# Output matmuls of a fused attention and maxout kernel issued as four column-tiled matmuls of 32 tokens

## The chip, the cores and the metric

The kernel runs on one core of one Trainium2 chip. The metric is the device time of one launch in microseconds (us), lower is better. The kernel before took 325.02 us, the median of two runs (324.05 and 326.00).

## The reference

Two stages over 4 batches of 12544 tokens with 128 channels, 32 inducing points and a maxout layer of width 1024 behind them:

```python
def mab(q, kv):
    s = scale * (q @ kv.transpose(0, 2, 1))
    s = s - s.max(-1, keepdims=True)
    a = np.exp(s)
    a /= a.sum(-1, keepdims=True) + 1e-09
    return a @ kv
h = mab(I, x)             # 32 inducing points attend to a batch's tokens
x2 = mab(x, h)            # each token attends to the 32 results
h1 = x2 @ w1
h2 = x2 @ w2
g = np.maximum(h1, h2)
out = g @ w_out           # (50176, 128), float32
```

## The kernel before

The tokens of a batch are cut into 98 chunks of 128. The kernel never forms x2. For each token it makes 32 unnormalised attention weights e (an exponential of scores), and since max(h1, h2) = h1 + max(h2 - h1, 0), the output is e times a small matrix (e @ (h w1 w_out), the "linear term") plus relu(e @ (h (w2 - w1))) @ w_out, all divided by the sum of the weights (the "denominator").

Work on TensorE (PE), in the names of the code:

- `stage` (L610): scores of up to 16 chunks at a time. Four chunks lie side by side in 32 partitions each, so these matmuls use 32 of the 128 columns of the array each, at `tile_position=(0, 32 * q)`: column-tiled. ScalarE (ACT) makes the exponential into a tile `e2`.
- `phase` (L1069): four matmuls (or a few more where they are narrow) that contract over 32 weights each, at `tile_position=(32 * q, 0)`: row-tiled, all four row strips at once. Each fills a bank with 512 columns of h2 - h1, which ACT (L1085) or VectorE (DVE, L1088) rectifies into a `relu` tile in f16. One of the four may be a linear term instead.
- `final_one` (L876): one output matmul, 128 tokens by 128 channels, contracting over 128 of the 1024 units. Its weights (stationary operand) are a 128x128 slice of a `relu` tile, its moving operand is a 128x128 slice of `w_out`. A chunk takes 8 of these, 3136 in all for 392 chunks. Up to four chunks share one bank of 512 columns. When a group is done, DVE scales it by the reciprocal denominators (`evict_group`, L907) and SyncE stores it by DMA.
- `linear_last` (L853): for a few groups ("full") the linear term comes after the output matmuls, one full-array matmul for each chunk.
- `dens` (L671): denominators, one matmul with 4 moving columns for each chunk column of a block. The later blocks get them from a DMA transpose and GpSimd instead.
- `keep_busy` (L833): idle matmuls on zeros, 256 columns each, that add nothing to the bank of a waiting group.
- `pool_scores` (L329) and `pool_accum` (L385, L404): the first attention of the next batch, also column-tiled. L385 is four matmuls side by side, each with 32 columns of weights and 128 moving columns.
- `pool_rest` (L351), `small_rep` (L430), `small_h` (L443), `small_hwd` (L505), `small_m1` (L518): a few matmuls over the full array for each batch.

The program's order on each engine is written out by a planner in the kernel itself: a `Clock` object holds an estimate of when PE, ACT, DVE and each of the 8 banks come free, with constants for an output matmul (0.0558 us) and for a change between full, row-tiled and column-tiled work, and a table of hand-made exceptions (`DEV`). The planner runs while the kernel is built. In the steady state a row-tiled phase and a run of some 13 to 16 output matmuls alternate. The first 25 us (the `HEAD` list) handle the first attention of batch 0 and contain no output matmul.

Of the kernel before, what the change touches and what calls it, by code (L numbers as in the profile page):

```python
# [102 lines left out]
def kernel(  # L103
# [9 lines left out]
    nc = tc.nc  # L113
# [28 lines left out]
    def bank(shape, dtype=F32, only=None):  # L142
        i = min(range(8), key=lambda j: ck.bank[j]) if only is None else only
        uid[0] += 1
        return i, psum.tile(shape, dtype, name=f"ps{uid[0]}", tag=f"bank{i}", bufs=1)
# [47 lines left out]
    repd = consts.tile([128, 128], F32, name="repd")  # L193
    diag = consts.tile([128, M], F32, name="diag")
    pace = consts.tile([128, 1], F32, name="pace")

    with tc.manual_schedule(engines={ET.PE, ET.DVE, ET.Activation, ET.Pool, ET.SP}):

# [457 lines left out]
        def dens(blk):  # L656

            blks = [blk]
            if 0 < blk.index < len(blocks) - 1:
                nxt = blocks[blk.index + 1]  # L660
                if nxt.staged is not None and nxt.staged <= ck.pe and nxt.rp is None and not nxt.turned:
                    blks.append(nxt)
            bi, ps = bank([128, 512])
            ck.wait(ck.bank[bi], "den bank")
            uid[0] += 1
            rp = rpp.tile([128, 8, 4], F32, name=f"rp_{uid[0]}", tag="rp")
            n = 0
            for blk in blks:
                wd = blk.width
                for t in range(wd):  # L670
                    nc.tensor.matmul(  # L671
                        out=ps[:, 4 * (n + t) : 4 * (n + t) + 4],
                        lhsT=blk.e2[:, 128 * t : 128 * (t + 1)],
                        rhs=ones_q,
                        start=True,
                        stop=True,
                    )
                blk.rp = rp[:, n : n + wd, :]
                n += wd
            end = ck.run(0.029 * n)  # L680
            nc.vector.reciprocal(out=rp[:, 0:n, :].rearrange("p t q -> p (t q)"), in_=ps[:, 0 : 4 * n])
            ck.bank[bi] = ck.on_dve(end, 0.18 + 0.001 * 4 * n)
# [138 lines left out]
        def keep_busy(until):  # L821

            g = groups[state["g"]] if state["g"] < len(groups) else None
            if held and held[0].full:
                g = held[0]
            elif g is None or g.ps is None or (g.full and state["mm"] == 0):
                return
            turn = ck.SWITCH["full"] if ck.mode != "full" else 0.0
            n = int((until - ck.pe - turn - 0.1) / 0.11)
            if n < (3 if turn else 1):  # L830
                return
            for _ in range(n):
                nc.tensor.matmul(  # L833
                    out=g.ps[:, 0:256],
                    lhsT=warm[:, 0:128],
                    rhs=warm[:, 0:256],
                    start=False,
                    stop=False,
                    skip_group_check=True,
                )  # L840
            ck.run(0.11 * n)

# [2 lines left out]
        def linear_last(end):  # L845

            while held:
                g = held[0]
                if g.full:
                    if st[g.blk.b].get("m1r", INF) > ck.pe:  # L850
                        return
                    for s, (q, t) in enumerate(g.chunks):
                        nc.tensor.matmul(  # L853
                            out=g.ps[:, 128 * s : 128 * (s + 1)],
                            lhsT=g.blk.e2[:, 128 * t : 128 * (t + 1)],
                            rhs=m1bd[:, q, :],
                            start=False,
                            stop=True,
                            skip_group_check=True,
                        )  # L860
                    end = ck.run(0.056 * len(g.chunks))
                evict_group(held.pop(0), end)

        def final_one():
            g = groups[state["g"]]
            n = len(g.chunks)
            if g.blk.rp is None and not g.blk.turned:
                dens(g.blk)
            if g.ps is None:
                g.bank, g.ps = bank([128, 512])  # L870
                ck.wait(ck.bank[g.bank], "group bank")
                ck.bank[g.bank] = INF
            jb, c = divmod(state["mm"], n)
            q, t = g.chunks[c]
            w4 = g.blk.quarters[q].w
            nc.tensor.matmul(  # L876
                out=g.ps[:, 128 * c : 128 * (c + 1)],
                lhsT=g.blk.relu[q][:, 128 * (jb * w4 + t) : 128 * (jb * w4 + t + 1)],
                rhs=woutp[:, jb, :],
                start=(g.full and state["mm"] == 0),  # L880
                stop=(jb == NJB - 1 and not g.full),
                skip_group_check=True,
            )
            end = ck.run(ck.PAIR)
            state["mm"] += 1
            state["done"] += 1
            if state["mm"] == n * NJB:
                held.append(g)
                linear_last(end)
                state["g"] += 1  # L890
                state["mm"] = 0
# [119 lines left out]
        def phase(jobs):  # L1011
# [6 lines left out]
            for (kind, q, a, u), bi in zip(jobs, free):  # L1018
                _, ps = bank([128, 512], only=bi)
                ready = max(ck.bank[bi], a.blk.staged if kind == "L" else a.staged)  # L1020
                if kind == "L":
                    ready = max(ready, st[a.blk.b]["m1r"])
                got.append((kind, q, a, u, bi, ps, ready))
            keep_busy(max(g[6] for g in got) - ck.SWITCH["row"])
            if ck.mode != "row":
                ck.pe += ck.SWITCH["row"]
# [221 lines left out]
        while state["g"] < len(groups) or held:  # L1248
# [3 lines left out]
            if held and ck.mode == "full":  # L1252
                linear_last(0.0)
# [19 lines left out]
            if tp < INF and lag() <= 128 + LIMIT and now:  # L1273
                if how != 3 and column_work(len(jobs) + 1, how == 4):
                    continue
                phase(jobs)
            elif tf < INF:
                keep_busy(tf)
                ck.wait(tf, "relu")
                final_one()  # L1280
            elif tp < INF:
                phase(jobs)
            elif pending:
                f, a = pending.pop(0)
                f(*a)
            else:
                raise AssertionError(("stuck", state, ptr, chunks_done, jobs, pending[:3]))
# [32 lines left out]
```

## Time and profile before

| what | value |
|---|---|
| times of the two runs | 324.05 us and 326.00 us, median 325.02 us |
| span of the profiled execution, first to last instruction | 322.5 us |
| median of the runs less that span (what lies around it) | 2.5 us |
| granted TensorE clock over the span | 1.000 |
| instructions with a record | 12605, of them 5375 matmuls and 5375 weight loads on PE |

The page gives the span of the profiled execution and not a separate time for it, so the 2.5 us set it beside the median of the runs. "PE" in the profile is the matmuls, "PEld" the weight loads that overlap them. A matmul is pipelined: its record of some 219 ns reaches from the start of its data to the modelled end, so records of neighbours overlap, and the spacing of matmuls is read from the difference of their starts. In a row of the timeline, a length less the length of one record is the time from the first start to the last start. Sources are lines of the kernel before.

### The profile page before, as it was taken

What the parts mean: (1) busy time and instruction counts of PE and PEld (TensorE: products, weight loads), DVE (VectorE), ACT (ScalarE), POOL (GpSimd) and SP (SyncE); (2) the same over time, 40 slices, a digit from 0 to 9 for tenths busy, and PEclk for the clock granted to TensorE, in tenths of its full rate; (3) what the DMA queues carried; (4) which work ended last, traced back from release to release, by engine and by line L of the source; (5) the groups of instructions that cost most, each with busy time, mean ns of one, the idle gap of its engine ahead of it and who ended that gap; (6) DMA issues with size and microseconds to landing.
All of it is one profiled execution on the core that took longest, in us unless ns stands there. A gap on an engine that the chain in (4) does not pass through costs nothing.

```text
span 322.5 us, 12605 instructions
## 1 busy us (share of the span) xinstructions
PE 315.6 (98%) x5375; PEld 239.8 (74%) x5375; DVE 281.4 (87%) x508; ACT 281.8 (87%) x561; POOL 37.8 (12%) x90
## 2 busy tenths in 40 slices
PE   7899999999999999999999999999999999999996
PEld 3776777777777777777777777777777777777786
DVE  3369999988989998999989989988998999899974
ACT  3779999998978999999898999998869999999960
POOL 7470000000040000000040000000006400302000
PEclk9999999999999999999999999999999999999999
DMA  8999999954279999794279999893424322324233
GB/s 205 207 268 213 218 249 203 210 136 133 100 150 245 221 254 216 181 194 139 99 151 242 218 258 207 160 211 120 118 96 103 135 80 100 109 100 128 87 118 116
DMA packets 77320, 53.99 MB, mean 167 GB/s; under 512 B 56112, under 2 KB 64976, under 8 KB 77264
## 3 DMA queue, kind: packets, MB, share of 16 engines
q1 hardware_dynamic: 71232, 39.42, 50.0%
q0 software_dynamic: 5888, 13.70, 21.7%
q8 instruction: 42, 0.69, 0.9%
q14 instruction: 14, 0.11, 0.1%
q10 hardware_dynamic: 144, 0.07, 0.1%
HBM read 27.28 MB, written 25.69 MB: 164 GB/s over the span
## 4 chain that ended last, share of the span: by engine, by line
PE 93%; DMA 5%; ACT 1%; issue 1%; POOL 0%; DVE 0%; POOLq 0%
PE ps L876 62%; PE ps L1069 22%; DMA xn<-in_x_dram 5%; PE ps L610 2%; PE ps L385 2%; PE ps L329 1%; PE ps L671 1%; PE ps L833 1%; ACT e L629 0%; PE ps L505 0%; ACT hwd L482 0%; PE ps L235 0%; PE ps L303 0%; PE ps L430 0%; PE ps L258 0%
## 5 line engine op out<-in xcount | busy, mean ns | idle before, releaser
L1085 ACT ACTIVATE relu<-ps 128x512 f16<-128x512 f32 x462 | 244.1, 604 | 23.0 <-PE ps L1069 15.0
L1088 DVE TENSOR_SCALAR relu<-ps 128x512 f16<-128x512 f32 x322 | 206.1, 682 | 16.2 <-PE ps L1069 14.8
L876 PE MATMUL ps<-woutp,relu 128*128 128x128 f16 x3136 | 216.9, 220 | 0.0
L876 PEld LDWEIGHTS <-relu 128*128 128x128 f16 x3136 | 176.6, 98 | 39.4 <-issue 28.9
L1069 PE MATMUL ps<-e,hwd 32*128 32x512 f16 (+2 forms) x888 | 88.2, 358 | 0.1
L907 DVE TENSOR_TENSOR o<-ps,rp 128x512 f32<-128x512 f32 (+3 forms) x80 | 51.2, 640 | 1.8 <-PE ps L876 1.3
L1069 PEld LDWEIGHTS <-hwd 32*128 32x128 f16 x888 | 24.5, 91 | 20.9 <-issue 0.8
L1069 PE MATMUL ps<-m,e 32*128 32x128 f16 x381 | 38.7, 217 | 0.0
L1069 PEld LDWEIGHTS <-e 32*128 32x128 f16 x381 | 21.2, 92 | 2.9 <-issue 0.4
L907 DVE TENSOR_TENSOR o<-ps,rpt 128x512 f32<-128x512 f32 (+3 forms) x28 | 17.3, 618 | 4.1 <-PE ps L853 2.2
L166 POOL DMA_DIRECT2D xn<-in_x_dram x33 | 17.8, 553 | 6.7 <-DMA xn<-in_x_dram 4.6
L164 POOL COPY pace<-hacc 128x1 f32<-128x1 f32 x2 | 0.4, 188 | 133.1 <-DVE hacc L418 133.1
L246 DVE COPY xT<-ps 128x768 f16<-128x768 f16 (+6 forms) x11 | 4.8, 458 | 8.9 <-PE ps L235 8.9
L340 ACT ACTIVATE eu<-ps 128x512 f16<-128x512 f32 x18 | 10.9, 614 | 0.1
L629 ACT ACTIVATE e<-ps 128x512 f16<-128x512 f32 (+2 forms) x21 | 10.4, 568 | 0.2 <-PE ps L610 0.2
L235 PE MATMUL ps<-identity,xn 128*128 128x128 f16 x98 | 8.1, 219 | 2.3 <-DMA xn<-in_x_dram 1.8
L535 POOL COPY m1bd<-m 32x128 f16<-32x128 f16 x4 | 1.1, 287 | 76.7 <-DVE m L530 76.6
L249 ACT COPY xT<-ps 128x768 f16<-128x768 f16 (+5 forms) x10 | 6.5, 671 | 3.0 <-PE ps L235 2.9
L698 POOL TENSOR_TENSOR w1T<-den 128x256 f32<-128x256 f16 (+1 forms) x7 | 4.4, 633 | 38.6 <-DMA den<-e 38.6
L700 POOL TENSOR_TENSOR w1T<-w1T 128x64 f32<-128x64 f32 (+4 forms) x28 | 8.4, 302 | 2.2
L235 PEld LDWEIGHTS <-xn 128*128 128x128 f16 x98 | 5.6, 97 | 4.0 <-DMA xn<-in_x_dram 2.2
L610 PE MATMUL ps<-xT,hT 128*32 128x512 f16 (+3 forms) x114 | 8.2, 361 | 0.0
(93 smaller groups left out, 117.0 us busy)
## 6 DMA issues: line engine op xcount, KB each, us to landing
out_dram<-o SPq DMA_DIRECT2D x68, 256.0 KB, 2.8
xn<-in_x_dram POOLq DMA_DIRECT2D x24, 448.0 KB, 10.1
out_dram<-o SPq DMA_DIRECT2D x54, 128.0 KB, 1.8
wf<-in_moe_w_dram POOLq DMA_DIRECT2D x4, 256.0 KB, 5.9
xn<-in_x_dram POOLq DMA_DIRECT2D x3, 224.0 KB, 8.8
xT<-xn SPq DMA_TRANSPOSE x42, 3.8
xf<-in_x_dram SPq DMA_DIRECT2D x1, 512.0 KB, 3.7
xf<-in_x_dram SPq DMA_DIRECT2D x1, 384.0 KB, 4.2
```

Source lines behind the costliest of these rows:

```text
L166: nc.gpsimd.dma_start(out=xn_at[b, i][lo:hi, 0:n, :], in_=xr[b, lo:hi, k0 : k0 + n, :])
L235: nc.tensor.transpose(ps[:, j, :], xn_at[0, i][:, g + j, :], identity16)
L249: nc.scalar.copy(out=dst, in_=ps[:, 0:m, :])
L340: nc.scalar.activation(out=eu, in_=ps, func=AF.Exp, scale=scale, accum_out=st[b]["es"][:, u : u + 1])
L610: nc.tensor.matmul(out=ps[32 * q : 32 * (q + 1), 128 * t : 128 * (t + n)], lhsT=hq, rhs=xT[:, c : c + n, :], start=True, stop=True, tile_p ...
L629: nc.scalar.activation(out=blk.e2[:, lo:hi], in_=ps[:, lo:hi], func=AF.Exp, scale=st[0]["rs"] if blk.b == 0 else scale,)
L700: nc.gpsimd.tensor_add(acc[:, :, 0:n], acc[:, :, 0:n], acc[:, :, n : 2 * n])
L876: nc.tensor.matmul(out=g.ps[:, 128 * c : 128 * (c + 1)], lhsT=g.blk.relu[q][:, 128 * (jb * w4 + t) : 128 * (jb * w4 + t + 1)], rhs=woutp[: ...
L907: nc.vector.tensor_mul(osb[:, 0:n, :], g.ps[:, 0 : n * C].rearrange("p (s c) -> p s c", s=n), rp)
L1069: nc.tensor.matmul(**seq[i])
L1085: nc.scalar.activation(out=dst, in_=src, func=AF.Relu)
L1088: nc.vector.tensor_scalar(out=dst, in0=src, scalar1=0.0, scalar2=None, op0=ALU.max)
```

## The change

A helper `by_columns` takes the place of `nc.tensor.matmul` at four places: the output matmul (L876), the late linear term (L853), the denominator (L671) and the idle matmul (L833). It issues four matmuls in place of one. Each takes 32 of the 128 weight columns (32 tokens), the whole moving operand, and writes 32 partitions of the same columns of the same bank. All matmuls of the four places carry `tile_position=(0, 32 * p)`. The planner's constants, the `DEV` table and everything on the other engines are left as they were.

```diff
+    def by_columns(out, lhsT, rhs, start, stop):
+
+        for p in range(4):
+            r = slice(32 * p, 32 * (p + 1))
+            nc.tensor.matmul(
+                out=out[r, :],
+                lhsT=lhsT[:, r],
+                rhs=rhs,
+                start=start,
+                stop=stop,
+                tile_position=(0, 32 * p),
+                skip_group_check=True,
+            )
...
-                    nc.tensor.matmul(
+                    by_columns(
                         out=ps[:, 4 * (n + t) : 4 * (n + t) + 4],
                         lhsT=blk.e2[:, 128 * t : 128 * (t + 1)],
                         rhs=ones_q,
...
-                nc.tensor.matmul(
+                by_columns(
                     out=g.ps[:, 0:256],
                     lhsT=warm[:, 0:128],
                     rhs=warm[:, 0:256],
                     start=False,
                     stop=False,
-                    skip_group_check=True,
                 )
...
-                        nc.tensor.matmul(
+                        by_columns(
                             out=g.ps[:, 128 * s : 128 * (s + 1)],
                             lhsT=g.blk.e2[:, 128 * t : 128 * (t + 1)],
                             rhs=m1bd[:, q, :],
                             start=False,
                             stop=True,
-                            skip_group_check=True,
                         )
...
-            nc.tensor.matmul(
+            by_columns(
                 out=g.ps[:, 128 * c : 128 * (c + 1)],
                 lhsT=g.blk.relu[q][:, 128 * (jb * w4 + t) : 128 * (jb * w4 + t + 1)],
                 rhs=woutp[:, jb, :],
                 start=(g.full and state["mm"] == 0),
                 stop=(jb == NJB - 1 and not g.full),
-                skip_group_check=True,
             )
```

## The prediction

> **What bounds the kernel now.** I read the page's busy line and chain of waits first, then the timeline of PE around 75 to 79 us, where all three kinds of tiling stand side by side, then the list by source for single lines. From the page:
>
> ```profile
> span 322.5 us, 12605 instructions
> PE 315.6 (98%) x5375; PEld 239.8 (74%) x5375; DVE 281.4 (87%) x508; ACT 281.8 (87%) x561; POOL 37.8 (12%) x90
> ...
> q8 instruction: 42, 0.69, 0.9%
> ...
> PE 93%; DMA 5%; ACT 1%; issue 1%; POOL 0%; DVE 0%; POOLq 0%
> ...
> L876 PE MATMUL ps<-woutp,relu 128*128 128x128 f16 x3136 | 216.9, 220 | 0.0
> ```
>
> PE is busy for 98% of the span and carries 93% of the chain that ends last, so what a PE step costs is paid in full, and what other engines do costs nothing while DVE and ACT have 13% to spare. The 3136 output matmuls waited for no data (the last 0.0). The timeline of PE (start, length, line, form, count):
>
> ```profile
> 74.71 0.40 PE L1069 MATMUL ps<-e,hwd 32*128 32x512 f16 x4
> 75.03 0.78 PEld L876 LDWEIGHTS <-relu 128*128 128x128 f16 x14 [0.23 <-issue]
> 75.03 0.95 PE L876 MATMUL ps<-woutp,relu 128*128 128x128 f16 x14
> 75.92 0.09 PEld L1069 LDWEIGHTS <-hwd 32*128 32x128 f16 x2
> ...
> 76.25 0.95 PE L876 MATMUL ps<-woutp,relu 128*128 128x128 f16 x14
> 77.14 0.10 PEld L1069 LDWEIGHTS <-hwd 32*128 32x128 f16 x4
> 77.14 0.40 PE L1069 MATMUL ps<-e,hwd 32*128 32x512 f16 x4
> 77.47 0.90 PEld L385 LDWEIGHTS <-eT 128*32 128x32 f16 x64 [0.23 <-issue]
> 77.47 1.08 PE L385 MATMUL ps<-xn,eT 128*32 128x128 f16 x64
> ...
> 78.47 0.28 PEld L876 LDWEIGHTS <-relu 128*128 128x128 f16 x5
> ```
>
> And by source:
>
> ```profile
> L385 PEld LDWEIGHTS <-eT x288: 92/97/97, 77.5 to 236.8; 128*32 128x32 f16 x144
> L385 PE MATMUL ps<-xn,eT x288: 219/219/230, 77.5 to 236.8; 128*32 128x128 f16 x144
> L385 PEldq EVENT_SEMAPHORE  x3: 51/51/51, 77.1 to 216.0; - x3
> ```
>
> The reader is to see two things. The kernel alternates: a row-tiled phase (L1069), a change of tiling, some 14 output matmuls, a change back, in about 1.2 us. And L385 is already the new form: four matmuls of 32 weight columns and 128 moving columns, side by side, f16, accumulating into one bank.
>
> **The change part by part.**
>
> *Output matmuls, 3136 to 12544.* Before: 14 of L876 start over 0.95 - 0.22 = 0.73 us, 13 gaps of 56 ns. After, by L385: 64 start over 1.08 - 0.22 = 0.86 us, which is 13.7 ns each if spread evenly, 55 ns for four; if the four of a quad start together, 15 gaps of 57 ns. So four cost what one costs, 56 ns, within about -1.5 and +1.0 ns. Times 3136 that is between -5 and +3 us; I take 0, since the same 128 columns stream. The quads differ from L385 in one respect: all four read the same moving operand at once, where each tile of L385 reads its own. No row shows that; I take it at nothing, as the addresses of L385's weights lie side by side in the same way and do no harm.
>
> The weight loads of L385 take 97 ns, those of L876 by the group list 98, and both start ahead of their matmuls; with four loads to a quad, 64 of them start over 0.90 - 0.10 = 0.80 us, in step with the matmuls.
>
> [...]
>
> *Changes of tiling.* From a phase's start to the first output matmul 75.03 - 74.71 = 0.32 us; to the first L385 77.47 - 77.14 = 0.33. From the last output matmul's start (75.03 + 0.73 = 75.76) to the next phase 0.16; from the last L385 (77.47 + 0.86 = 78.33) to the next load of L876 0.14, with a quad's own skew in front. So no change of tiling becomes cheaper or dearer by more than the 0.01 us of the rows. In the order of PE's instructions I count 476 changes before and 478 after: some 30 between column-tiled work and output matmuls go away, since these are now one mode, and some 30 come new around the full-array steps (L351, L430, L443, L505, L518). At 0.32 - 0.22 = 0.10 us each (four times 56 ns is the stream of 512 columns) the two more cost 0.2 us. The fourth matmul of a quad starts a little after the first, so each of the 221 runs ends later by 0 to 0.01 us: 0 to 2.2, I take 1.1 us.
>
> *Denominators, 76 to 304.* The list by line and timelines of three spots:
>
> ```profile
> L671 PE MATMUL ps<-ones_q,e 128*128 128x4 f16 x76 | 3.5, 165 | 0.1
> ```
> ```profile
> 24.92 0.24 PE L671 MATMUL ps<-ones_q,e 128*128 128x4 f16 x4
> ```
> ```profile
> 88.31 0.22 PE L404 MATMUL ps<-xn,et 128*32 128x128 f16 x2
> 88.31 0.17 PE L404 MATMUL ps<-ones,warm 128*32 128x1 f16 x2
> 88.36 0.17 PE L404 MATMUL ps<-ones,et 128*32 128x1 f16 x2
> ```
>
> One denominator now costs (0.24 - 0.164) / 3 = 25 ns. A quad costs between the same 25 (all four side by side) and 56 (a full quad): 0 to 2.4 us over 76. The nearest row is L404, short column-tiled matmuls 50 ns apart: 76 x 25 = 1.9 us, which I take.
>
> *Late linear terms (11) and idle matmuls (13).* These keep their 128 and 256 moving columns, by the quad argument 0. The idle ones fill a wait that exists anyway.
>
> *What supplies the instructions.* PE had 2 x 5375 loads and matmuls. 3136 + 76 + 11 + 13 = 3236 pairs become 12944, so PE now gets 2 x 15083 = 30166, one each 10.7 ns over the span against 30 ns before; in a run of quads, 8 in 56 ns, one each 7 ns. The work that could hide a slow supply is a queue of instructions ahead of the array. The row that bears on it is the semaphore instruction of L385: it waits in PE's queue directly ahead of the first load, at 77.1 us for 0.05. The burst's 128 instructions were therefore handed over between 77.15 and the start of its last load, 77.47 + 0.80 = 78.27: at most 1.1 us / 128 = 9 ns each, and the array never starved. A steady run looks the same: the phase ahead of it gives 0.32 us of lead, then come 13 to 16 quads, as many as L385's 16. At the 9 ns bound a run gains a delay of 72 - 56 = 16 ns for each quad beyond about 16. I take 0.
>
> *Everything else.* No instruction of DVE, ACT, GpSimd or SyncE moves and no DMA is added but fetches of instructions (0.69 MB to about 1.9 MB, 0.9% to 2.6% of the queues' time). A wait on a relu tile or a bank is now met by the first of four, and the scaling of a group waits for the last; both stand within 10 ns of before.
>
> *Sum.* 0 + 0.2 + 1.1 + 1.9 = 3.2 us on a span of 322.5, so 325.7; with the 2.5 us between span and median, **328.2 us**. The bounds of these terms alone are -5 + 0 + 0 + 0 and +3 + 2.2 + 2.2 + 2.4, so 320 to 335; quads at the ends of that are less likely than in the middle, so the own range of this case is 323 to 332.
>
> **The rivals.**
>
> *Supply at the bound.* If an instruction costs 9 ns, runs over 16 quads lose 16 ns a quad. The chain's long runs show the amount:
>
> ```profile
> 306.19 1.78 PE ps L876 x30
> 309.19 2.34 PE ps L876 x40
> 313.96 2.45 PE ps L876 x42
> ```
>
> These three alone lose (14 + 24 + 26) x 16 ns = 1 us; with the rest, and runs at the edge, I put 4 us: 332 us. For it: 9 ns is all that is shown. Against: L385 shows no sag.
>
> *Loads or issue limited to 25 ns a pair.* L671 shows pairs 25 ns apart where there is nothing to stream. If 25 ns is what a pair costs in the long run, and L385 only looks faster because its 128 instructions were queued, then after the first 25 us (385 matmuls there) 14698 pairs take 367 us: about 25 + 367 + 2.5 = 395 us. Against: 13.7 ns held through 64 pairs, behind a semaphore that barred queueing earlier than 0.3 us before. [...]
>
> *Fetching the instructions.* 42 blocks of 16 KB become about 118, one each 2.7 us instead of 7.7. A block's packet takes 0.009 x 16 x 322.5 / 42 = 1.1 us. If PE holds only one block ahead and a fetch takes longer than 2.7 us from request to landing where the queues are full, PE stalls; a transfer of 256 KB takes 2.8 us to land and loads of x far longer:
>
> ```profile
> out_dram<-o SPq DMA_DIRECT2D x68, 256.0 KB, 2.8
> xn<-in_x_dram POOLq DMA_DIRECT2D x24, 448.0 KB, 10.1
> ```
>
> Between nothing and a whole packet of stall for each block (118 x 1.1 = 130 us), I put 20 us: 348 us. Against: the stall needs a shallow buffer and a slow fetch at once. No row shows how many blocks are held. [...]
>
> *Cheaper changes of tiling* (faster than before). If the array need not drain between row-tiled and column-tiled work, the 0.10 us at each of 441 changes shrinks. From 15 ns each this is worth 6.6 us and decides; at half the change, 22 us: 306 us. Against: L1069 to L385 and back already is such a change and costs 0.33 and 0.14 us, like that to the full array.
>
> **How the numbers follow.** Equal quads 0.68 at 328.2; supply at the bound 0.12 at 332; fetching 0.10 at 348; 25 ns a pair 0.07 at 395; cheaper changes 0.03 at 306. About 2%, some 6.5 us, is what a measurement of this kernel can tell from no change, so "slower" begins at 331.5: all of the 25 ns case, 0.08 of fetching, 0.07 of the supply case and 0.08 of the forecast's upper tail, 0.30; faster 0.03; the rest 0.67. The range from 323 to 345 leaves out the 25 ns case, half of fetching and about 0.05 below.
>
> **What would show it.** Right: PE quads 56 ns apart in runs of 14 (0.73 us from first to last start), a phase still 0.16 us behind the last quad, denominators near 50 ns, PE near 98% busy, no idle time ahead of matmuls. Wrong: a run of 14 quads lasting over 1 us (supply or loads; the first quads at 56 and later ones wider means supply), single gaps of a microsecond spread over the span, about 118 packets on the instruction queue each followed by a gap (fetching), or phases starting sooner behind a quad than 0.14 us (cheaper changes).

## The result and the profile after

The changed kernel takes 488.74 us (median of two runs, 486.33 and 491.15) against 325.02 us: 1.50 times as long (95% interval 1.484 to 1.525). The forecast was 328.2 us with a range up to 345. From the page of the changed kernel (L201 is the helper's matmul, L1080 the row-tiled phase):

```profile
span 489.2 us, 32021 instructions
...
PE 357.0 (73%) x15083; PEld 259.9 (53%) x15083; DVE 290.1 (59%) x508; ACT 288.1 (59%) x561; POOL 38.3 (8%) x90
...
PEclk8999999999978999999957999999999999999989
...
q8 instruction: 117, 1.92, 1.7%
...
PE 66%; issue 25%; DMA 5%; DVE 2%; ACT 1%; POOL 1%; SPq 0%; POOLq 0%; DVEq 0%
...
L201 PE MATMUL ps<-woutp,relu 128*32 128x128 f16 x12544 | 250.1, 226 | 100.8 <-issue 100.7
```

PE was busy for 98% of its span and is busy for 73%. A quarter of the chain that ends last is "issue": PE waits for nothing that the profile can name. The matmuls of the quads carry 100.8 us of idle time, where the output matmuls had 0.0. The clock, at full speed all through before, shows a few slices under 9. In the timeline of PE the idle time has a shape:

```profile
58.65 0.62 PE L201 MATMUL ps<-woutp,relu 128*32 128x128 f16 x30
60.21 0.57 PE L201 MATMUL ps<-woutp,relu 128*32 128x128 f16 x26 [0.94 <-issue]
60.72 0.23 PE L1080 MATMUL ps<-m,e 32*128 32x128 f16 x1
60.72 0.39 PE L1080 MATMUL ps<-e,hwd 32*128 32x512 f16 x3
60.78 0.33 PE L1080 MATMUL ps<-m,e 32*128 32x128 f16 x3
61.04 0.96 PE L201 MATMUL ps<-woutp,relu 128*32 128x128 f16 x56
61.94 0.40 PE L1080 MATMUL ps<-e,hwd 32*128 32x512 f16 x4
62.26 0.40 PE L624 MATMUL ps<-xT,hT 128*32 128x512 f16 x4
62.49 0.39 PE L343 MATMUL ps<-xT,inducingT 128*32 128x512 f16 x4
62.70 0.56 PE L201 MATMUL ps<-woutp,relu 128*32 128x128 f16 x27
64.77 0.24 PE L201 MATMUL ps<-woutp,relu 128*32 128x128 f16 x4 [1.50 <-issue]
```

Two things are to be seen. The run at 61.04 is healthy: 56 matmuls, 14 quads, start within 0.96 - 0.22 = 0.74 us, as the 14 output matmuls did before (0.73). And the stalls cut runs at odd places, behind 30 matmuls and behind 27, in the middle of a quad. The rows between the stalls count 26 + 7 + 56 + 4 + 4 + 4 + 27 = 128 matmuls. Two windows, from the end of one stall to the start of the next and over that next stall, say the same with the weight loads. Behind the window stand its length, the busy times of PE, PEld, DVE, ACT and POOL, each with a count of instructions, the granted clock, the DMA share and GB/s:

```profile
60.20:63.10 2.90, 2.89 (x128) 2.12 (x128) 1.96 (x4) 1.94 (x5) 0.00 (x0) 1.00 1.48 182
63.10:64.70 1.60, 0.17 (x13) 0.00 (x0) 0.58 (x1) 1.50 (x4) 0.00 (x0) 1.00 0.65 128
```

128 matmuls and 128 loads are 256 instructions, at the full clock (1.00). The instruction queue moved packets of 16 KB (1.92 MB / 117), and one packet for 256 instructions would be 64 bytes for each. The trace's records give every gap over 0.45 us between starts of PE's instructions (loads, matmuls and the few semaphore and drain instructions, in order of start): 107 of them fall on the same place, behind number 192 in each 256 (counted from 0), and together they hold 139 us beyond 0.1 us each. Eleven fall elsewhere.

The instruction queue's packets show how a stall ends. Medians over these 107: the first instruction of a block runs; 1.17 us later a packet starts (the fetch of the next block); it takes 1.12 us on average; 1.39 us behind its end (1.24 to 1.53 for nine in ten) the next block's first instruction starts. By these figures one turn is 1.17 + 1.12 + 1.39 = 3.7 us. Some packets start later (1.50 us on average), so the measured time from block to block is longer, 4.00 us at the median and 4.05 on average: 117 such turns are 474 of the 489 us. The work of 256 instructions at the quads' density takes about 2.9 us (the first window), so PE idles in nearly every block. Before, a block's work took 322.5 / 42 = 7.7 us and the whole turn lay under it: each packet ended at least 2.3 us ahead of the first instruction of its block. In no kernel of this case does a block start sooner than 1.1 us behind its own packet.

### The profile page after: what moved, and what is told of

The parts are those of the page before. It is cut to its first block, busy times and chain, and to the rows that moved or that the text cites. A ratio compares the mean times of both kernels' runs of the same rounds, so it can differ in the third digit from the quotient of the medians.

```text
span 489.2 us, 32021 instructions
## 1 busy us (share of the span) xinstructions
PE 357.0 (73%) x15083; PEld 259.9 (53%) x15083; DVE 290.1 (59%) x508; ACT 288.1 (59%) x561; POOL 38.3 (8%) x90
## 3 DMA queue, kind: packets, MB, share of 16 engines
q8 instruction: 117, 1.92, 1.7%
## 4 chain that ended last, share of the span: by engine, by line
PE 66%; issue 25%; DMA 5%; DVE 2%; ACT 1%; POOL 1%; SPq 0%; POOLq 0%; DVEq 0%
PE ps L201 46%; PE ps L1080 16%; DMA xn<-in_x_dram 2%; DMA wf<-in_moe_w_dram 1%; PE ps L399 1%; PE ps L624 1%; DVE relu L1099 1%; DMA xT<-xn 1%; DMA out_dram<-o 1%; PE ps L343 1%; POOL xn L166 1%; ACT relu L1096 1%; DVE o L918 0%; PE ps L519 0%; ACT eu L354 0%
## 5 line engine op out<-in xcount | busy, mean ns | idle before, releaser
L1096 ACT ACTIVATE relu<-ps 128x512 f16<-128x512 f32 x462 | 248.8, 598 | 169.3 <-PE ps L1080 161.9
L201 PE MATMUL ps<-woutp,relu 128*32 128x128 f16 x12544 | 250.1, 226 | 100.8 <-issue 100.7
L1099 DVE TENSOR_SCALAR relu<-ps 128x512 f16<-128x512 f32 x322 | 209.8, 684 | 131.0 <-PE ps L1080 129.1
L201 PEld LDWEIGHTS <-relu 128*32 128x32 f16 x12544 | 193.0, 99 | 153.6 <-issue 141.0
L1080 PE MATMUL ps<-e,hwd 32*128 32x512 f16 (+2 forms) x888 | 94.1, 374 | 11.2 <-issue 4.4
L1080 PEld LDWEIGHTS <-hwd 32*128 32x128 f16 x888 | 25.8, 92 | 35.1 <-issue 17.2
L1080 PE MATMUL ps<-m,e 32*128 32x128 f16 x381 | 40.3, 223 | 1.7 <-issue 1.6
L1080 PEld LDWEIGHTS <-e 32*128 32x128 f16 x381 | 21.9, 94 | 6.5 <-issue 4.1
L399 PE MATMUL ps<-xn,eT 128*32 128x128 f16 x288 | 6.5, 227 | 4.3 <-issue 4.3
```

What stands on the lines that cost most here:

```text
L201: nc.tensor.matmul(out=out[r, :], lhsT=lhsT[:, r], rhs=rhs, start=start, stop=stop, tile_position=(0, 32 * p), skip_group_check=True,)
L399: nc.tensor.matmul(out=ps[32 * g : 32 * (g + 1), 0:128], lhsT=eT[:, j, 32 * g : 32 * (g + 1)], rhs=xn_of(b, U * v + 4 * g + j), start=(j = ...
L1080: nc.tensor.matmul(**seq[i])
L1096: nc.scalar.activation(out=dst, in_=src, func=AF.Relu)
L1099: nc.vector.tensor_scalar(out=dst, in0=src, scalar1=0.0, scalar2=None, op0=ALU.max)
```

## The experiments

Theory 1 is that loop: PE holds one block of 256 instructions ahead, and a block can be used about 3.7 us (the sum above; 4.0 measured) after the one ahead of it was entered. Rival A: column tiling itself is dear, some 53 ns a quad (167 us over 3136 output matmuls). Rival B: every added instruction costs alike, 8.6 ns. "Blocks" below is the count of packets on the instruction queue, "stalls" that of the gaps over 0.45 us at the block's edge, in one profiled execution of each kernel. The counts of loads and matmuls are the trace's; those in the expectations are 13 lower.

| kernel | loads and matmuls | blocks | time, us | stalls, and us in them |
|---|---|---|---|---|
| before | 10750 | 42 | 325 | 0 |
| rest alone | 11350 | 44 | 328.33 | 0 |
| one of four runs | 15586 | 61 | 334.52 | 7, 6 |
| halves, no columns | 17022 | 66 | 342.64 | 8, 12 |
| two tiles of 64 | 17222 | 67 | 345.66 | 5, 9 |
| every second run | 20224 | 79 | 365.10 | 22, 29 |
| three of four runs | 25330 | 98 | 426.98 | 73, 83 |
| no columns, many instructions | 28552 | 111 | 467.06 | 97, 109 |
| few stores | 30166 | 117 | 485.11 | 105, 133 |
| the change | 30166 | 117 | 488.74 | 107, 139 |

**Many instructions without column tiles.** Each output matmul is cut by its moving columns, and phases are cut too:

```diff
-            nc.tensor.matmul(
-                out=g.ps[:, 128 * c : 128 * (c + 1)],
-                lhsT=g.blk.relu[q][...],
-                rhs=woutp[:, jb, :],
+            for h in range(2):
+                nc.tensor.matmul(
+                    out=g.ps[:, 128 * c + 64 * h : 128 * c + 64 * (h + 1)],
+                    lhsT=g.blk.relu[q][...],
+                    rhs=woutp[:, jb, 64 * h : 64 * (h + 1)],
...
+                parts_[n] = [
+                    dict(m, out=m["out"][:, x : x + 64], rhs=m["rhs"][:, x : x + 64], ...)
+                    for m in seq
+                    for x in range(0, m["out"].shape[1], 64)
+                ]
```

> No column tiling at the four places (all as before the change), but nearly as many instructions as the changed kernel has: each output matmul is two full-array matmuls of 64 moving columns that load the same weights twice, and the matmuls of a row-tiled phase are cut into pieces of 64 columns. Nothing is left out. 28539 loads and matmuls on PE. Worked from the spacing of pairs (56 ns for 128 columns, no pair under 25 ns) the array's own work grows by about 11 us. Theory 1 (fetch): 450 to 475 us, with stalls at every 256th instruction as in the changed kernel. Rival A (column tiling itself): 325 + 11 = 336 us, up to 345. Rival B (8.6 ns for each of 17802 added instructions): 478 us.

Measured 467.06 us (one run). From its page (L877 the halves, L1076 the phases):

```profile
span 465.3 us, 30448 instructions
...
q8 instruction: 111, 1.82, 1.7%
...
PE 72%; issue 22%; DMA 2%; ACT 1%; DVE 1%; POOL 1%; POOLq 0%; DVEq 0%
...
L877 PE MATMUL ps<-woutp,relu 128*128 128x64 f16 x6272 | 242.2, 196 | 47.2 <-issue 47.2
```

The same picture without a quad at the four places: "issue" is 22% of the chain, and 97 stalls fall behind number 192 of each 256, though the mix of instructions is another. Rival A, which gave 336 to 345 us, is out as the cause. Rival B had nearly the same number here, 478 us; two tiles and quads in part of the runs, below, separate it.

**Two tiles of 64 tokens.** Still column-tiled, half the instructions:

```diff
-        for p in range(4):
-            r = slice(32 * p, 32 * (p + 1))
+        for p in range(2):
+            r = slice(64 * p, 64 * (p + 1))
...
-                tile_position=(0, 32 * p),
+                tile_position=(0, 64 * p),
```

> Two column tiles of 64 tokens in place of four of 32 at all four places: still column-tiled, 17209 loads and matmuls on PE in place of 30153 (before: 10737). Theory 1, instruction fetch: PE gets its instructions in blocks of 256, holds one block ahead and needs about 3.7 us from entering a block until the next but one can be used (as the regular stalls of the changed kernel show, one every 256 instructions, resumed about 1.4 us behind the block's packet). A block here lasts about 4.8 us of work, so no stall: 325 to 329 us, and no idle time of microseconds on PE. Rival A, column tiling itself costs about 53 ns for an output matmul (167 us of longer span / 3236 quads; half of it with half the tiles): about 407 us, with half 366 us. Rival B, every added instruction costs alike, 167 us / 19416 = 8.6 ns: 325 + 6472 x 8.6 ns = 381 us.

Measured 345.66 us, 1.064 times before (1.058 to 1.069). Rivals A and B are 20 us and more too high, but my range ended 17 us too low. The page and a stall in the timeline:

```profile
PE 328.6 (96%) x8611; PEld 251.8 (73%) x8611; DVE 283.8 (83%) x508; ACT 282.6 (82%) x561; POOL 38.3 (11%) x90
...
PEclk9699999999999899999999989999999999999999
DMA  8999999965289999994279976879632422333233
```
```profile
40.16 0.41 PE L201 MATMUL ps<-woutp,relu 128*64 128x128 f16 x8
43.18 0.75 PE L201 MATMUL ps<-woutp,relu 128*64 128x128 f16 x20 [2.61 <-issue]
```

Five stalls at a block's edge remain, at 40, 110, 184, 189 and 196 us: all in slices (8.6 us each) where the DMA line shows 9. There a fetch comes late: in the trace's records these five packets start 3.0 to 4.8 us after the first instruction of the block ahead of them, where the median packet of this kernel starts after 0.6. Late packets coincide with loads: of its 66 packets 10 start more than 2.3 us late, all of them while GpSimd's queue (q0), which loads x and the weights, has packets in flight, and only two packets are in time beside such traffic. In the kernel before, 6 of 41 packets are as late, all beside such traffic too, but there a block's work is long enough to hide it. The stalls hold 9.3 us. The clock was at half speed for 6.8 us in the first 25 us, where the first output matmul starts only about 1 us later than before, and for twice 3.4 us later, which cost some 3 us with PE busy throughout. The first output matmul after a change of tiling is followed by the second after 80 ns rather than 66: 3 us over 220 runs. And 29 more changes of tiling, 505 against 476, are 3 us at 0.10 us each. Together these are some 18 of the 21 us by which the span grew (343.9 - 322.5); the rest was not traced.

**Quads in part of the runs.** A counter in `phase` picks four tiles or one full-array matmul for a whole run, so the phases stay as they are:

```diff
     def by_columns(out, lhsT, rhs, start, stop):
+        if not (run[0] % 2):
+            nc.tensor.matmul(out=out, lhsT=lhsT, rhs=rhs, start=start, stop=stop, skip_group_check=True)
+            return
...
         def phase(jobs):
+            run[0] += 1
```

> Four column tiles as in the changed kernel, but only in every second run between two row-tiled phases; the other runs use one full-array matmul as before. No change of tiling is added or removed at a phase. 20211 loads and matmuls on PE. Theory 1 (fetch): a run with quads and one without hold together about 160 instructions in 2.45 us, so a block of 256 lasts 3.9 us, just over the 3.7 us of the fetch loop: few and short stalls, 330 to 342 us. Rival A (53 ns for each quad, half the quads): 407 us. Rival B (8.6 ns for each of 9474 added instructions): 406 us.

Measured 365.10 us, 1.125 times before (1.120 to 1.130), 41 us under both rivals and 23 us above the range of theory 1: 22 stalls with 29 us, and 14 us at half clock. The mean of 3.9 us a block is itself just under the 4.0 us that a turn was measured to take in the changed kernel, and it hides that one block may lie in a dense stretch and the next in a thin one, and that fetches come late while x is loaded: 9 of the 22 stalls stand behind a packet that is more than 2.3 us late. With `run[0] % 4` in place of `run[0] % 2`:

> As the one before, but quads in three of four runs: 25317 loads and matmuls on PE. Theory 1 (fetch): a block lasts 3.1 us of work, less than the loop of 3.7 to 3.85 us; each of about 97 blocks stalls for some 0.7 us, plus what the lowered clock adds: 390 to 420 us. Rival A: 325 + 0.75 x 167 = 450 us. Rival B: 325 + 14580 x 8.6 ns = 450 us.

Measured 426.98 us (one run), 7 us over the range; 450 is refuted with 23 us to spare. And quads in only one of four runs (`if run[0] % 4:`):

> Four column tiles in one of four runs between phases, full-array matmuls in the others: 15573 loads and matmuls on PE. Theory 1 (fetch): a block of 256 lasts 5.5 us of work, well over the loop of 3.7 us, so stalls are rare, 325 to 333 us. Rival A (53 ns for each of 784 + 100 quads): 372 us. Rival B (8.6 ns for each of 4836 added instructions): 367 us.

Measured 334.52 us, 1.027 times before (1.025 to 1.030), 1.5 us above the range: 7 short stalls, 6 us, even at 5.5 us a block; their packets start 3.0 to 3.8 us after the block ahead of them began. All seven start while q0 has packets in flight. A straight price for each quad or instruction would have given 372 or 367.

**Halves without column tiles**, the first part of the cut above alone, to set beside the two tiles:

> No column tiling at the four places; each output matmul is two full-array matmuls of 64 moving columns, the phases are as before. 17009 loads and matmuls on PE, about as many as the kernel with two tiles of 64 tokens has (17209). Nothing is left out. The array's own work grows by 2 to 3 ns for each output matmul, 6 to 9 us. Theory 1 (fetch): a few late fetches while x is loaded, as with two tiles (5 stalls, 9 us, and some 6 us by the lowered clock): 335 to 352 us. Rival A (column tiling itself): no stall, 331 to 334 us. Rival B (8.6 ns for each of 6272 added instructions): 379 us and more.

Measured 342.64 us, 1.053 times before (1.050 to 1.056), the median of three executions; a fourth took 348.07 us, and it is the one whose stalls the table counts. That is within the range of theory 1, 9 us above rival A's and 36 us under rival B's. Nearly the same count of instructions with and without column tiles gives nearly the same time, though not by the same parts: here an output matmul takes 58.3 ns in place of 55.8, 8 us over 3136, and no change of tiling is added.

**Denominators, late linear terms and idle matmuls alone** as quads, output matmuls as before:

> Output matmuls as before the change; only denominators (76), late linear terms (11) and idle matmuls (13) are four column tiles. 11337 loads and matmuls on PE, so no block of instructions is short of time. The new changes of tiling (denominators lie in full-array runs, some 20 groups, in and out) cost 20 to 40 times 0.1 us. Theory 1 (fetch): nothing beyond that and the 1.9 us of the denominators, 326 to 331 us. Rival A (a column-tiled quad costs 53 ns by itself): 100 x 53 ns = 5 us more, 331 to 336 us.

Measured 328.33 us, 1.009 times before (1.0075 to 1.011), no stall. Its PE order has 508 changes of tiling, 32 more than before; at 0.10 us they are 3.2 us, all of the difference, which leaves nothing for the denominators. A row of its timeline:

```profile
25.64 0.26 PE L201 MATMUL ps<-ones_q,e 128*32 128x4 f16 x16
```

16 of them start within 0.26 - 0.166 = 0.09 us, 6 ns each, 25 ns a quad: what one took before.

**Fewer stores.** The changed kernel, with seven of eight groups of results left unstored:

> The changed kernel, but only every eighth group of results (and the last one) is stored to HBM; the other stores are left out, about 22 MB of the 55 MB that the queues move. Nothing else differs. It tells whether the fetch loop of 3.7 us is long because other transfers are in its way. If the loop is mostly fixed (1.1 us from the request to the packet, 0.9 us for an undisturbed packet, 1.3 us until the first instruction), it falls to about 3.5 us and the time to 465 to 483 us. If the stores' traffic makes it long, the loop falls under 2.7 us and the time to 340 to 400 us.

Measured 485.11 us (one run), just above the range. The packets take 1.08 us in place of 1.12, and the median time from block to block falls from 4.00 to 3.75 us. So the loop is mostly fixed, and the stores make it somewhat longer; the loads of x were all left in.

## Why the prediction was wrong

- *Changes of tiling:* 478 against 476 and 0.10 us each. The 32 added changes of "rest alone" come with 3 us; right.
- *Output matmuls, equal quads:* right as a price of the array. Four tiles that read the same moving operand kept the 56 ns; 14 quads in 0.74 us. Their weight loads took 97 ns at the median, those of L876 before 98.
- *Denominators, 1.9 us:* wrong and without weight. The quads lay at the lower end, 25 ns ("rest alone").
- *What supplies the instructions, "I take 0":* the step that failed. The 9 ns an instruction were read from one burst of 128 instructions, half a block. They bound how fast PE takes over instructions that are already beside it, and there 7 ns hold (8 in the 56 ns of a quad), but not how fast new ones arrive. The sum needed a second bound over hundreds of instructions: 256 in 4.0 us, 15.6 ns each. The program wanted one each 10.7 ns on average.
- *Fetching, a rival at 0.10:* right in place and mechanism, even in the shape that was to show it, a packet and a gap for each block. It expected the stall where the queues are full; it came in nearly every block, also with 22 MB of stores left out. At a stall no further block was at hand: the next one began 1.39 us behind its own packet, and that packet started only 1.17 us after the block ahead was entered (medians). It was mis-sized: I put 20 us, within bounds of 0 to 130. The stalls hold 139 us, more than the upper bound, which left out the 1.4 us between a packet's end and the first instruction and the 1.2 us ahead of the packet. The row of DMA landings that I quoted, 2.8 us from issue to landing for stores of 256 KB, already stood above the 2.7 us that a block would last on average. A store is not a fetch, but the row was a reason to give this case more than 0.10.
- *The clock:* not in the prediction. It was at half speed for 44.4 us of the span, 41.0 of them behind the first output matmul, and PE was busy for about 35 of these. Quads then stood 107 ns apart, so some 17 us were lost. Stalls and this make 156 of the 167 us by which the span grew; the last 10 or so I did not trace.

## What to carry to other kernels

Count an engine's instructions as a resource of its own: on PE here 256 of them could be had in about 4.0 us. That is 64 a microsecond. The four kernels of the table with 73 to 107 stalls would have needed 79 to 94 a microsecond to keep the span of 322.5 us; the one with 15586 loads and matmuls in 333 us, 47 a microsecond, had 7 stalls, where the fetches came late beside loads of x. Splitting a matmul into tiles that run side by side kept the array's time here and multiplied the instructions, so it had nothing to gain and a fetch to pay for. Tiles that take the place of several small matmuls add no instructions; no run here shows what they gain. The short burst of L385 in the trace, at most 9 ns an instruction, showed what the array can do, not what was kept up, 15.6 ns: look for the count of instructions between stalls, and for a constant one.

## What the runs showed of the hardware

- The place of a stall went with the instruction's number, not with its kind: it was behind 192 of 256 in each of the eight kernels of the table that stalled, with 5 to 107 stalls.
- Stalls cost again: in the changed kernel the granted clock fell to half in pieces of 3.4 us or multiples of it (6.8, 17.1). Behind the first 25 us each such piece followed 3.4 us in which PE was idle for 51% to 78%, by one or two stalls, the longest of them 2.0 to 3.7 us. Work ran at 107 ns a quad meanwhile.
- Packets on the instruction queue started later while GpSimd's queue had loads in flight: in the kernel with two tiles more than 2.3 us after the block ahead was entered, in 10 of the 12 blocks with such traffic, against 0.6 us at the median.
- Column-tiled matmuls of 4 moving columns started 6 ns apart on average ("rest alone"), those of 128 columns 14 ns (the changed kernel), where full-array matmuls of 4 columns did not come closer than 25 ns (before).
